# Attention with a linear memory, and a layer of experts: one PSUM bank per head for the joint outputs, two transposes in later slots, and an operand updated in place

## The chip, the core and the metric

The program runs on one core of a Trainium2 chip. The metric is the device time of one execution in microseconds. All matrix products take fp32r operands that are split into a high and a low part, so a product of two fp32 matrices is three matmuls (high·high, high·low, low·high).

## The reference

```python
# q, k, v: [4, 8, 576, 64]; M_prev: [4, 8, 64, 64]; z_prev: [4, 8, 64]
scores = where(causal, -1e9, scale * q @ k.T)
a = softmax(scores)
local = a @ v
q_p = phi(q)                                   # elu(q) + 1
mem_out = (q_p @ M_prev) / (q_p @ z_prev + 1e-6)
g = sigmoid(beta)
x = (g * mem_out + (1 - g) * local)            # -> [2304, 512], heads side by side
p = domain_probs / sum(domain_probs)
out = sum over 4 experts e of p[:, e] * (relu(x @ w1[e]) @ w2[e])   # w1: 512x1024
```

## The kernel before

The attention's rows are cut into chunks of 128 queries (the fifth has 64). A task is one pair of heads of one batch with a run of chunks. Four tasks of batch 0 come first, written out by hand; then come twelve **joint** tasks (batches 1 to 3, four head pairs, chunks 0 and 1), and sixteen tasks of the other chunks (2, 3, 4). A task's steps are called events: `t_trq` and `t_trk` transpose queries and keys on TensorE into a PSUM tile (`tq`, `tk`), `t_trqp` phi of the queries (`tp`), and each is followed by ScalarE and VectorE instructions that write the high and low halves (qa, qb, kha, khb, kl, qpa, qpb); `j_qk` makes the scores (tile `sp`), `j_norm` normalizes, `j_pt` transposes the probabilities (`pt`) and writes their high half with ScalarE (line 604) and low half with VectorE (line 605); `j_o` makes the output (`o`) from phi, the memory `ms`, the probabilities and `v`; `o_out` adds its two halves into the tile `xr`, which holds x.

Meanwhile TensorE works on the experts, with the x that is there: `mm1` (line 968) makes `h`, whose relu is split into `hh` (ScalarE) and `hl` (VectorE, line 978), and `mm2` (line 1000) makes `y`, which VectorE adds into `acc`. The weights of each phase are split by `w_prep`: w2's high half on ScalarE, its low half `w2l` on GpSimd (line 227). These products are cut into parts; a planner puts the events between the parts. Each event has a slot and a priority in a table, and a weight worked out from its cost on TensorE and VectorE; a joint task has four slots, the others five. So the order of a slot's events is by priority, and how many product parts stand between two events goes by the weights.

PSUM tiles come from pools with a few banks per tag, taken in turn: a new tile waits until the instructions that read the tile that had the bank are done. Tag "to" has two banks; `tq`, `tk`, `tp`, the outputs `o`, and at the end two operands of the last pass use them. "qk" has two, "pt" one, "moe" three.

The last pass over the remaining rows computes its products by a scheme with differences of x: `x_steps` makes the operands t1 = x1 − x0, t2 = x3 − t1, t4 = x2 − t2 and t3 = x3 − x1 with `diff`, two halves each, and splits each into high and low (lines 1089 and 1092). They are made while the phase before the pass still runs.

Of the kernel before, what the change touches and what calls it, by code (L numbers as in the profile page):

```python
# [8 lines left out]
F32 = mybir.dt.float32  # L9
# [17 lines left out]
    "trq": [-3, 6.5],  # L27
    "trk": [-4, -0.5],
    "v": -2,
    "trqp": [2, 2.5, -1],  # L30
    "qk": 0,
    "exp": 6.5,
    "norm": 2.3,
# [2 lines left out]
    "jn": [1, -0.5],  # L36
    "jp": [2, 6.4],
    "jo": [3, 11],
    "wpe": 0.5,
    "wvec": 100.0,  # L40
    "frac": 0.97,
# [8 lines left out]
def tile_attention_moe(  # L50
# [13 lines left out]
    nc = tc.nc  # L64
# [542 lines left out]
    def j_o(i):  # L607
        s = slots[i]
        t = s.t
        o = to_tile(f"o{i}").rearrange("p (h q) -> p h q", h=2)  # L610
        for hd in range(2):
            hs = slice(2 * hd, 2 * hd + 2)
            ms = bdat[t.run][2][:, t.a, hs].rearrange("p j d -> p (j d)")
            qp = t.qk["qpa" if hd == 0 else "qpb"]
            nc.tensor.matmul(o[:, hd], lhsT=ms, rhs=qp[:, 0:GW], start=True, stop=False)  # L615
            for x in "hl":
                for j in range(2):
                    vs = t.v[:, j, hs].rearrange("p j d -> p (j d)")
                    nc.tensor.matmul(  # L619
                        o[:, hd, j * P :],  # L620
                        lhsT=vs,
                        rhs=s.p4[x][:, hd, j, j * P :],
                        start=False,
                        stop=j == 1 and x == "l",
                    )
        o_out(t, i, [(0, o[:, 0]), (1, o[:, 1])])

    def o_out(t, i, os_):

        tmp = att.tile([P, NQ], F32, tag="otmp", name=f"otmp{i}", bufs=1)  # L630
        lohi = (slice(0, D), slice(D, P))
        for h, o in os_:
            nc.scalar.activation(tmp[lohi[h], 0 : t.nq], o[lohi[1 - h], 0 : t.nq], AF.Copy)
        if not t.joint:
            a = 3 * P - t.q0
            for h, o in os_:
                x = lohi[h]
                nc.vector.tensor_tensor(
                    tmp[x, a : t.nq], o[x, t.nq : 2 * t.nq - a], tmp[x, a : t.nq], ALU.add
                )  # L640
        runs = []
        for c in t.cs:
            r, a, n = rcol(t.b, c), c * P - t.q0, rows(c)
            if runs and runs[-1][0] + runs[-1][2] == r:
                runs[-1][2] += n
            else:
                runs.append([r, a, n])
        for h, o in os_:
            x = lohi[h]
            for r, a, n in runs:  # L650
                nc.vector.tensor_tensor(
                    xr[x, t.a, r : r + n], o[x, a : a + n], tmp[x, a : a + n], ALU.add
                )

    def s_qk(i):
        s = slots[i]
# [126 lines left out]
    def s_o(i):  # L783
        s = slots[i]
        t = s.t
        pt = PT[s.hd]
        o = to_tile(f"o{i}")
        hs = slice(0, 2) if s.hd == 0 else slice(2, 4)
        ms = bdat[t.run][2][:, t.a, hs].rearrange("p j d -> p (j d)")
        qp = t.qk["qpa" if s.hd == 0 else "qpb"]  # L790
        nc.tensor.matmul(o[:, 0 : t.nq], lhsT=ms, rhs=qp[:, 0 : t.nq], start=True, stop=False, skip_group_check=True)  # L791
        vs = [t.v[:, j, hs].rearrange("p j d -> p (j d)") for j in range(t.nk)]
        a3 = 3 * P - t.q0
        o3 = o[:, a3 : 2 * t.nq - a3].rearrange("p (z q) -> p z q", z=2)
        for x, j in (("h", 0), ("h", 1), ("h", 2), ("h", 4), ("l", 0), ("l", 1), ("hl", 3), ("l", 2)):
            a = max(0, j * P - t.q0)
            nc.tensor.matmul(  # L797
                o3 if j == 3 else o[:, a : t.nq],
                lhsT=vs[j],
                rhs=PTB[s.hd][:, :, 3, a:] if j == 3 else pt[x][:, j, a : t.nq],  # L800
                start=False,
                stop=j == 3 or (x, j) == ("l", 2),
                skip_group_check=True,
            )
        o_out(t, i, [(s.hd, o)])

    def mm(n):
        return max(107.0, n / 2.4 + 2.5)
# [7 lines left out]
    def dv(n):  # L816
        return 150.0 + n / 0.96

    seen = set()
    for t in tasks:  # L820
        s0 = t.s0
        ld = -9 + t.i if t.i < 2 else s0 - 7
        PQ = PR
        n = len(t.cs)
        if t.run not in seen:
            seen.add(t.run)
            ev(s0 - 9, 9 if t.i else 6, lambda r=t.run: batch_load(r))
            ev(s0 - (5 if t.i else 8), 9, lambda r=t.run: batch_load_m(r))
            ev(s0 + (2 if t.joint else 3), 9 if t.joint else 0.1, lambda r=t.run: batch_prep(r))
            if t.cs == CB and t.b == 0:  # L830
                for i in range(2):
                    ev(s0 - 12, 9, lambda i=i: zeros(i))
        if t.joint:
            ev(ld, 6.3, lambda t=t: t_load(t))
        else:
            ev(s0 - 8, 8, lambda t=t: t_load(t, "qk"))
            ev(s0 - 6, 8, lambda t=t: t_load(t, "v"))
        if t.i:
            p1, p2 = (PQ["phi1"], PQ["phi2"]) if t.i > 1 else ((-4, 6.75), (-4, 7))
            ev(s0 + p1[0], p1[1], lambda t=t: t_phi1(t))  # L840
            ev(s0 + p2[0], p2[1], lambda t=t: t_phi2(t), 0.0, dv(n * P))
        ev(
            s0 + (PQ["phi3"][0] if t.i > 1 else (0, -3)[t.i]),
            PQ["phi3"][1] if t.i > 1 else (6.6, 19)[t.i],
            lambda t=t: t_phi3(t),
            0.0,
            600.0 if t.joint else 750.0,
        )
        ev(s0 - 3 if t.i else s0, 20 if t.i else 6.7, lambda t=t: t_phi4(t))
        if t.i == 0:  # L850
            ev(s0 - 1, 5, lambda t=t: t_trq(t), 109.0 * n, 2 * dv(n * P))
        else:
            ev(s0 + PQ["trq"][0], PQ["trq"][1], lambda t=t: t_trq(t), 109.0 * n, 2 * dv(n * P))
            ev(
                s0 + PQ["trk"][0],
                PQ["trk"][1],
                lambda t=t: t_trk(t),
                109.0 * (t.nk - t.k0),
                2 * dv((4 - t.k0) * P),
            )  # L860
        if not t.joint:
            ev(s0 + PQ["trq"][0] + 1, 0.5, lambda t=t: t_cpq(t))
            ev(s0 + PQ["trk"][0], 2.4, lambda t=t: t_cpk(t))
        if t.joint:
            ev(s0 + 1, 9, lambda t=t: t_keep(t))
        elif t.b:
            ev(s0 + PQ["trk"][0], 2.3, lambda t=t: t_take(t))
        ev(s0, PQ["v"], lambda t=t: t_v(t))
        ev(
            s0 + PQ["trqp"][0 if t.joint else 2],  # L870
            PQ["trqp"][1],
            lambda t=t: t_trqp(t),
            109.0 * n,
            2 * dv(t.nq),
        )
    for i, s in slots.items():
        w = wid(s.c)
        t = s.t
        if t.joint:
            ev(i, PQ["qk"], lambda i=i: j_qk(i), 4 * mm(w), 2 * dv(w) + 160)  # L880
            ev(i, PQ["exp"], lambda i=i: j_exp(i))
            ev(i + PQ["jn"][0], PQ["jn"][1], lambda i=i: j_norm(i), 0.0, 2 * dv(w) + 700)
            ev(i + PQ["jp"][0], PQ["jp"][1], lambda i=i: j_pt(i), 218.0 * (s.c + 1), dv(2 * w))
            if i in t.end:
                ev(
                    i + PQ["jo"][0],
                    PQ["jo"][1],
                    lambda i=i: j_o(i),
                    6 * mm(GW) + 4 * mm(P),
                    2 * dv(GW),  # L890
                )
            continue
        ev(i, PQ["qk"], lambda i=i: s_qk(i), 2 * mm(w) if w <= 512 else 6 * mm(w // 2), dv(w))
        ev(i, PQ["exp"], lambda i=i: s_exp(i))
        ev(i + 1, PQ["norm"], lambda i=i: s_norm(i), 0.0, 1000.0 if s.c > 2 else 400.0)
        if s.c == 2:
            ev(i + 1, 6.45, lambda i=i: s_scale(i))
        ev(i + 2, PQ["pt"], lambda i=i: s_pt(i), 109.0 * min(s.c + 1, 4), dv(min(w, 512)))
        if s.c == 4:
            ev(i + 2, PQ["pt"] + 0.1, lambda i=i: s_pt(i, True), 109.0, 400.0)  # L900
        if i in t.end:
            cost = mm(t.nq) + sum(2 * mm(t.nq - max(0, j * P - t.q0)) for j in range(t.nk))
            ev(i + 3, PQ["o"], lambda i=i: s_o(i), cost, 600.0)
# [177 lines left out]
    def x_steps():  # L1081
# [10 lines left out]
            eng.tensor_tensor(x[n][1][:, c], src(), f(x[n][0][:, c]), ALU.subtract)  # L1092

        def diff(n, c, tag, a, b_):
            t_[n, c] = ps.tile([P, 512], F32, tag=tag, name=f"{n}_{c}", bufs=2)
            nc.vector.tensor_tensor(t_[n, c], a(), b_(), ALU.subtract)

        V, G = nc.vector, nc.gpsimd
# [24 lines left out]
        both(D_, "t4", "qk", 2, "t2")  # L1123
        both(L_, "t2", "t2", V)
        both(H_, "t4", "t4")
        both(D_, "t3", "to", 3, 1)
        both(L_, "t4", "t4", V)
        both(H_, "t3", "t3")
        both(L_, "t3", "t3", V)
# [660 lines left out]
```

## Time and profile before

| what | value |
| --- | --- |
| time, median of 3 runs | 975.38 us (975.23 to 976.3) |
| the profiled execution: its time | 975.54 us |
| its span in the trace | 973.8 us |
| TensorE busy | 967.5 us (99%) |
| VectorE busy | 663.0 us (68%) |
| ScalarE busy | 569.6 us (58%) |
| GpSimd busy | 591.1 us (61%) |

The profile comes from one execution; its span in the trace is a little shorter than its time. Shares are of the span. Matmuls are pipelined, so their durations overlap: what one costs is read from the distance between the starts of neighbours.

### The profile page before, as it was taken

What the parts mean: (1) busy time and instruction counts of PE and PEld (TensorE: products, weight loads), DVE (VectorE), ACT (ScalarE), POOL (GpSimd) and SP (SyncE); (2) the same over time, 40 slices, a digit from 0 to 9 for tenths busy, and PEclk for the clock granted to TensorE, in tenths of its full rate; (3) what the DMA queues carried; (4) which work ended last, traced back from release to release, by engine and by line L of the source; (5) the groups of instructions that cost most, each with busy time, mean ns of one, the idle gap of its engine ahead of it and who ended that gap; (6) DMA issues with size and microseconds to landing.
All of it is one profiled execution on the core that took longest, in us unless ns stands there. A gap on an engine that the chain in (4) does not pass through costs nothing.

```text
span 973.8 us, 16241 instructions
## 1 busy us (share of the span) xinstructions
PE 967.5 (99%) x5018; PEld 815.2 (84%) x5018; DVE 663.0 (68%) x1791; ACT 569.6 (58%) x1393; POOL 591.1 (61%) x621
## 2 busy tenths in 40 slices
PE   9999999999999999999999999999999999999998
PEld 6889888888888899888888888888888888888887
DVE  7888888889888788888888877834324243342533
ACT  7888776776766779766666675643424334242430
POOL 7999856765674668865557455676255372554720
PEclk9999999999999999999999999999999999999999
DMA  8679655654444267644535332242111111111102
GB/s 193 187 186 225 163 160 142 175 146 110 116 126 126 65 185 201 178 124 115 131 106 134 94 95 64 64 130 60 50 44 55 54 55 55 44 55 47 51 1 87
DMA packets 187815, 107.04 MB, mean 110 GB/s; under 512 B 90704, under 2 KB 167632, under 8 KB 187728
## 3 DMA queue, kind: packets, MB, share of 16 engines
q1 hardware_dynamic: 186608, 105.73, 40.1%
q8 instruction: 40, 0.66, 0.3%
q14 instruction: 47, 0.39, 0.1%
q10 hardware_dynamic: 1088, 0.26, 0.1%
q0 software_dynamic: 32, 0.00, 0.0%
HBM read 93.23 MB, written 8.13 MB: 104 GB/s over the span
## 4 chain that ended last, share of the span: by engine, by line
PE 97%; DVE 1%; POOL 1%; DMA 1%; issue 0%; ACT 0%; SPq 0%; POOLq 0%
PE y L1000 23%; PE h L968 22%; PE y L1277 18%; PE x L1199 9%; PE z L1199 5%; PE pt L364 4%; PE sp L678 4%; PE o L797 4%; PE y L1199 2%; PE o L619 1%; PE tp L364 1%; PE tq L364 1%; PE tk L364 1%; PE sp L533 1%; PE o L791 0%; PE o L615 0%
## 5 line engine op out<-in xcount | busy, mean ns | idle before, releaser
L227 POOL TENSOR_TENSOR w2l<-stg,w2h 128x512 fp32r<-128x512 f32 x128 | 167.5, 1316 | 149.1 <-ACT w2h L224 144.7
L968 PE MATMUL h<-xh,w 128*128 128x512 f32 (+1 forms) x768 | 243.9, 368 | 0.0
L227 POOL TENSOR_TENSOR w<-stg,w 128x512 fp32r<-128x512 f32 x96 | 124.9, 1308 | 141.8 <-ACT w L224 132.3
L968 PEld LDWEIGHTS h<-xh,w 128*128 128x128 f32 x768 | 138.7, 189 | 17.8 <-issue 0.2
L968 PE MATMUL h<-xl,w 128*128 128x512 f32 (+1 forms) x384 | 136.3, 355 | 0.0
L1000 PE MATMUL y<-w2h,hh 128*128 128x512 f32 x320 | 134.4, 420 | 0.0
L1000 PE MATMUL y<-w2h,hl 128*128 128x512 f32 x320 | 126.1, 394 | 0.2 <-DVE hl L978 0.2
L1000 PE MATMUL y<-w2l,hh 128*128 128x512 f32 x320 | 125.7, 393 | 0.3 <-POOL w2l L227 0.3
L1294 DVE SCALAR_TENSOR_TENSOR acc<-y,pn,acc 128x512 f32<-128x512 f32 (+1 forms) x57 | 41.6, 740 | 82.2 <-PE y L1277 82.2
L735 ACT ACTIVATE pt<-pt 128x384 fp32r<-128x384 f32 (+3 forms) x128 | 50.2, 420 | 62.8 <-PE pt L364 61.2
L968 PEld LDWEIGHTS h<-xl,w 128*128 128x128 f32 x384 | 72.8, 190 | 5.8
L1000 PEld LDWEIGHTS y<-w2h,hl 128*128 128x128 f32 x320 | 60.0, 188 | 14.0 <-DVE hl L978 0.6
L977 ACT ACTIVATE hh<-h 128x512 fp32r<-128x512 f32 (+1 forms) x96 | 50.3, 524 | 29.2 <-PE h L968 27.7
L1000 PEld LDWEIGHTS y<-w2l,hh 128*128 128x128 f32 x320 | 60.5, 189 | 8.1 <-POOL w2l L227 1.1
L1000 PEld LDWEIGHTS y<-w2h,hh 128*128 128x128 f32 x320 | 60.3, 188 | 7.8
L737 DVE TENSOR_TENSOR pt<-pt,pt 128x384 fp32r<-128x384 f32 (+3 forms) x128 | 57.3, 468 | 11.0 <-ACT pt L735 9.7
L978 DVE SCALAR_TENSOR_TENSOR hl<-h,hh 128x512 fp32r<-128x512 f32 (+1 forms) x96 | 57.5, 599 | 10.3 <-ACT hh L977 9.1
L364 PE MATMUL pt<-ident,s 128*128 128x128 f32 (+1 forms) x376 | 60.8, 272 | 0.2
L1223 DVE TENSOR_TENSOR cp_a<-y,cp_a 128x512 f32<-128x512 f32 x16 | 11.1, 692 | 71.4 <-PE y L1199 71.4
L364 PEld LDWEIGHTS pt<-ident,s 128*128 128x128 f32 (+1 forms) x376 | 46.9, 139 | 14.2 <-issue 0.5
L224 ACT ACTIVATE w<-stg 128x512 fp32r<-128x512 f32 x92 | 57.0, 625 | 0.8
L1016 DVE SCALAR_TENSOR_TENSOR acc<-y,pn,acc 128x512 f32<-128x512 f32 x70 | 52.3, 747 | 5.9 <-PE y L1000 5.0
(291 smaller groups left out, 2503.7 us busy)
## 6 DMA issues: line engine op xcount, KB each, us to landing
stg<-in_moe_w_dram SPq DMA_DIRECT2D x256, 256.0 KB, 3.0
natall<-in_v_dram SPq DMA_DIRECT2D x32, 128.0 KB, 3.4
natall<-in_q_dram SPq DMA_DIRECT2D x60, 64.0 KB, 3.0
out_dram<-acc SPq DMA_DIRECT2D x15, 256.0 KB, 2.1
natall<-in_k_dram SPq DMA_DIRECT2D x52, 64.0 KB, 2.4
zb<-in_z_prev_dram SPq DMA_DIRECT2D x7, 256.0 KB, 4.2
mr<-in_M_prev_dram SPq DMA_DIRECT2D x14, 128.0 KB, 3.2
natall<-in_v_dram SPq DMA_DIRECT2D x24, 64.0 KB, 2.4
```

The lines of the kernel that those rows point to most:

```text
L224: nc.scalar.activation(hi, t, AF.Copy)
L227: nc.gpsimd.tensor_tensor(lo, t, f(hi), ALU.subtract)
L364: nc.tensor.transpose(dst, src, ident[0:n, 0:n])
L735: nc.scalar.activation(dh, src, AF.Copy)
L737: nc.vector.tensor_tensor(dl, src, f(dh), ALU.subtract)
L968: nc.tensor.matmul(pt[0][:, cols], lhsT=w_[:, c], rhs=x_[:, c, cols], start=(c == 0 and z == 0), stop=(c == NKD - 1 and z == 2),)
L977: nc.scalar.activation(h_, pt[0][:, cols], AF.Relu)
L978: nc.vector.scalar_tensor_tensor(l_, pt[0][:, cols], 0.0, f(h_), ALU.max, ALU.subtract)
L1000: nc.tensor.matmul(pt[0], lhsT=h_[fc][:, tk], rhs=w_, start=(fc == 0 and z == 0), stop=(fc == HF - 1 and z == 2),)
L1016: nc.vector.scalar_tensor_tensor(acc[g, tt], pt[0], pe, acc[g, tt], ALU.mult, ALU.add)
L1199: nc.tensor.matmul(k_, lhsT=w_[:, c], rhs=x_[:, c], start=new and n == 0, stop=n == 5, skip_group_check=True,)
L1277: nc.tensor.matmul(y0, lhsT=a[:, tk], rhs=w_[:, x0:x1], start=(fc == 0 and z == 0), stop=(fc == HF - 1 and z == 2),)
```

## The change

It has three parts. `j_o` takes a "to" bank for each head (o{i}_0, o{i}_1) where both heads had one bank. In a head's bank, columns 0 to 255 hold the memory product and chunk 0's values times the high, then the low half of the probabilities; for chunk 1 the high and the low half stand side by side in one operand of 256 columns, whose product goes to columns 128 to 383. So there are four matmuls of 256 columns for each head instead of three of 256 and two of 128, and an add on VectorE joins the last 128 columns to the rest. `o_out` is called for each head. `t_trq` of the joint tasks goes from slot −3, priority 6.5, to slot −2, priority 1, counted from the task's first slot, and their `t_trqp` from slot +2 to slot +3. In `x_steps`, t3 is made as t2 − x0 in t2's own PSUM bank, instead of x3 − x1 in a bank of its own.

```diff
-    "trqp": [2, 2.5, -1],
+    "trqp": [-1, 2.5],
+    "jtrq": [-2, 1],
+    "jtrqp": [3, 2.5],
...
     def j_o(i):
...
-        o = to_tile(f"o{i}").rearrange("p (h q) -> p h q", h=2)
+        both = PTB[t.i % 2].rearrange("p z j q -> p z (j q)")
+        tmp = o_tmp(i)
         for hd in range(2):
+            o = to_tile(f"o{i}_{hd}")
...
-            nc.tensor.matmul(o[:, hd], lhsT=ms, rhs=qp[:, 0:GW], start=True, stop=False)
-            for x in "hl":
-                for j in range(2):
-                    vs = t.v[:, j, hs].rearrange("p j d -> p (j d)")
-                    nc.tensor.matmul(
-                        o[:, hd, j * P :],
-                        lhsT=vs,
-                        rhs=s.p4[x][:, hd, j, j * P :],
-                        start=False,
-                        stop=j == 1 and x == "l",
-                    )
-        o_out(t, i, [(0, o[:, 0]), (1, o[:, 1])])
+            v0, v1 = (t.v[:, j, hs].rearrange("p j d -> p (j d)") for j in range(2))
+            c1 = (2 * hd + 1) * GW + P
+            o1 = o[:, P : P + GW].rearrange("p (z q) -> p z q", z=2)
+            for n, (dst, w_, x_) in enumerate(
+                (
+                    (o[:, 0:GW], ms, qp[:, 0:GW]),
+                    (o[:, 0:GW], v0, s.p4["h"][:, hd, 0]),
+                    (o1, v1, both[:, :, c1 : c1 + P]),
+                    (o[:, 0:GW], v0, s.p4["l"][:, hd, 0]),
+                )
+            ):
+                nc.tensor.matmul(
+                    dst, lhsT=w_, rhs=x_, start=n == 0, stop=n > 1, skip_group_check=True
+                )
+            o_out(t, hd, o, tmp)
...
-        if not t.joint:
-            a = 3 * P - t.q0
...
+        a = P if t.joint else 3 * P - t.q0
+        nc.vector.tensor_tensor(
+            tmp[x, a : t.nq], o[x, t.nq : 2 * t.nq - a], tmp[x, a : t.nq], ALU.add
+        )
...
-                    6 * mm(GW) + 4 * mm(P),
-                    2 * dv(GW),
+                    8 * mm(GW),
+                    2 * dv(GW) + 2 * dv(P),
...
         def diff(n, c, tag, a, b_):
-            t_[n, c] = ps.tile([P, 512], F32, tag=tag, name=f"{n}_{c}", bufs=2)
+            if tag:
+                t_[n, c] = ps.tile([P, 512], F32, tag=tag, name=f"{n}_{c}", bufs=2)
+            else:
+                t_[n, c] = a()
             nc.vector.tensor_tensor(t_[n, c], a(), b_(), ALU.subtract)
...
-        both(D_, "t3", "to", 3, 1)
+        both(D_, "t3", None, "t2", 0)
```

How the order moves is seen best in three places. The first is TensorE's order where the joint tasks end: the tile tq is that of the first task with three chunks (its three transposes), o the output of the eleventh joint task, h the experts' first product. Before:

```order
L364 MATMUL tq_2920<-ident,natall 128x128 x3
L968 MATMUL h_0_2901<-xh,w_111 128x512
L968 MATMUL h_0_2901<-xl,w_111 128x512
L968 MATMUL h_0_2901<-xh,w_111 128x512
L615 MATMUL o_2957<-qpa_84,ms_0_2440 128x256
L619 MATMUL o_2957<-pt_98,v_2652 128x256
L619 MATMUL o_2957<-pt_98,v_2652 128x128
L619 MATMUL o_2957<-pt_98,v_2652 128x256
L619 MATMUL o_2957<-pt_98,v_2652 128x128
L615 MATMUL o_2957<-qpb_85,ms_0_2440 128x256
L619 MATMUL o_2957<-pt_98,v_2652 128x256
```

And of the change:

```order
L366 MATMUL tq_2946<-ident,natall 128x128 x3
L972 MATMUL h_1_2935<-xh,w_111 128x512
L972 MATMUL h_1_2935<-xl,w_111 128x512
L972 MATMUL h_1_2935<-xh,w_111 128x512 x2
L972 MATMUL h_1_2935<-xl,w_111 128x512
L972 MATMUL h_1_2935<-xh,w_111 128x512
L630 MATMUL o_0_2987<-qpa_84,ms_0_2444 128x256
L630 MATMUL o_0_2987<-pt_98,v_2675 128x256 x3
L630 MATMUL o_1_2995<-qpb_85,ms_0_2444 128x256
L630 MATMUL o_1_2995<-pt_98,v_2675 128x256 x3
```

The output now stands six products behind tq instead of three, has eight matmuls, and takes two tiles, o_0 and o_1, right behind tq in the tag's turn.

The second place is TensorE's order at the output of the second joint task; tq is that of a later joint task. Before:

```order
L968 MATMUL h_3_1121<-xh,w_111 128x256
L968 MATMUL h_3_1121<-xl,w_111 128x256
L968 MATMUL h_3_1121<-xh,w_111 128x256
L364 MATMUL tq_1131<-ident,natall 128x128 x2
L968 MATMUL h_3_1121<-xh,w_111 128x256
L968 MATMUL h_3_1121<-xl,w_111 128x256
L968 MATMUL h_3_1121<-xh,w_111 128x256 x2
L968 MATMUL h_3_1121<-xl,w_111 128x256
L968 MATMUL h_3_1121<-xh,w_111 128x256 x2
L968 MATMUL h_3_1121<-xl,w_111 128x256
L968 MATMUL h_3_1121<-xh,w_111 128x256
L615 MATMUL o_1156<-qpa_93,ms_0_763 128x256
```

And of the change:

```order
L972 MATMUL h_3_1122<-xh,w_111 128x256
L972 MATMUL h_3_1122<-xl,w_111 128x256
L972 MATMUL h_3_1122<-xh,w_111 128x256
L630 MATMUL o_0_1139<-qpa_93,ms_0_753 128x256
L630 MATMUL o_0_1139<-pt_99,v_795 128x256 x3
L630 MATMUL o_1_1147<-qpb_94,ms_0_753 128x256
L630 MATMUL o_1_1147<-pt_99,v_795 128x256 x3
L972 MATMUL h_3_1122<-xh,w_111 128x256
L972 MATMUL h_3_1122<-xl,w_111 128x256
L972 MATMUL h_3_1122<-xh,w_111 128x256 x2
```

The transposes of tq are no longer ahead of the output (they stand among later products), and the output comes eight rows earlier in the expert products of h_3.

The third is VectorE's order where the operands of the last pass are made; t2, t3 and t4 are PSUM tiles, each with its half's number, and t2l and t4l the low halves. Before:

```order
L1092 TENSOR_TENSOR t2l_8274<-t2_0_8339,t2h_8273 128x512
L1092 TENSOR_TENSOR t2l_8274<-t2_1_8344,t2h_8273 128x512
L978 SCALAR_TENSOR_TENSOR hl2_109<-h23_2_8381,hh2_105 128x512
L1096 TENSOR_TENSOR t3_0_8412<-xr_100 128x512
L1096 TENSOR_TENSOR t3_1_8417<-xr_100 128x512
L1092 TENSOR_TENSOR t4l_8280<-t4_0_8372,t4h_8279 128x512
```

And of the change:

```order
L1096 TENSOR_TENSOR t2l_8286<-t2_0_8351,t2h_8285 128x512
L1096 TENSOR_TENSOR t2l_8286<-t2_1_8356,t2h_8285 128x512
L982 SCALAR_TENSOR_TENSOR hl2_109<-h23_2_8393,hh2_105 128x512
L1103 TENSOR_TENSOR t2_0_8351<-t2_0_8351,xr_100 128x512
L1103 TENSOR_TENSOR t2_1_8356<-t2_1_8356,xr_100 128x512
L1096 TENSOR_TENSOR t4l_8292<-t4_0_8384,t4h_8291 128x512
```

The two subtractions stand at the same place; they now read and write t2's tile where they read two pieces of xr.

## Rows read from the trace of the kernel before

**Rows 1.** The head of the page: the span, busy time by engine, granted TensorE clock
```profile
span 973.8 us, 16241 instructions
...
PE 967.5 (99%) x5018; PEld 815.2 (84%) x5018; DVE 663.0 (68%) x1791; ACT 569.6 (58%) x1393; POOL 591.1 (61%) x621
...
PEclk9999999999999999999999999999999999999999
```

**Rows 2.** TensorE's waits: us in total, times, longest
```profile
PE ids L1610 <- DVE hh L1656: 1.5, 1, 1.5
PE y L1000 <- POOL w2l L227: 0.3, 1, 0.3
```

**Rows 3.** Timeline of TensorE, 63.3 to 66.5: start, duration, line, tiles
```profile
63.50 0.28 PE L615 MATMUL o<-qpa,ms 128*128 128x256 f32 x1
...
64.62 0.45 PE L1000 MATMUL y<-w2h,hh 128*128 128x512 f32 x1
64.91 0.40 PE L1000 MATMUL y<-w2l,hh 128*128 128x512 f32 x1
65.14 0.40 PE L1000 MATMUL y<-w2h,hl 128*128 128x512 f32 x1
...
66.07 0.28 PE L533 MATMUL sp<-kha,qa 128*128 128x256 f32 x1
66.19 0.28 PE L533 MATMUL sp<-qz,qa 128*128 128x256 f32 x1
```

**Rows 4.** Line 615: ns min/median/max, first and last start
```profile
L615 PE MATMUL o<-qpa,ms x12: 277/282/283, 49.6 to 207.2; 128*128 128x256 f32 x12
```

**Rows 5.** Timelines of GpSimd and TensorE, 47 to 62
```profile
47.64 5.08 POOL L227 TENSOR_TENSOR w2l<-stg,w2h 128x512 fp32r<-128x512 f32 x4
...
49.00 0.50 PE L1000 MATMUL y<-w2l,hh 128*128 128x512 f32 x1 [0.27 <-POOL w2l L227]
...
52.82 0.45 PE L1000 MATMUL y<-w2l,hh 128*128 128x512 f32 x1
...
61.41 1.30 POOL L227 TENSOR_TENSOR w2l<-stg,w2h 128x512 fp32r<-128x512 f32 x1
```

**Rows 6.** Timelines of TensorE, ScalarE and VectorE, 189.5 to 194.2
```profile
189.94 0.49 PE L364 MATMUL tq<-ident,natall 128*128 128x128 f32 x3
...
190.96 0.28 PE L615 MATMUL o<-qpa,ms 128*128 128x256 f32 x1
...
190.47 0.38 ACT L376 ACTIVATE qa<-tq 64x256 fp32r<-64x256 f32 x1 [1.73 <-PE tq L364]
...
192.24 0.42 DVE L380 SCALAR_TENSOR_TENSOR qa<-tq,qa 64x256 fp32r<-64x256 f32 x1 [1.00 <-ACT khb L390]
...
193.81 0.23 DVE L396 TENSOR_TENSOR kl<-tq,khb 64x64 fp32r<-64x64 f32 x1
```

**Rows 7.** The tile otmp, instructions by line
```profile
L638 DVE TENSOR_TENSOR otmp<-o,otmp x32: 340/355/361, 227.5 to 616.1; 64x192 f32<-64x192 f32 x32
```

**Rows 8.** Timelines of TensorE and VectorE behind the first two chunk-1 transposes
```profile
43.92 0.87 PE L364 MATMUL pt<-ident,s 128*128 128x128 f32 x4
...
46.87 0.69 DVE L605 TENSOR_TENSOR pt<-pt,pt 128x512 fp32r<-128x512 f32 x1
...
59.26 0.60 PE L364 MATMUL pt<-ident,s 128*128 128x128 f32 x4
...
61.77 0.69 DVE L605 TENSOR_TENSOR pt<-pt,pt 128x512 fp32r<-128x512 f32 x1 [1.05 <-ACT pt L604]
```

**Rows 9.** Timelines of VectorE and TensorE, 622 to 635
```profile
622.65 1.28 DVE L1096 TENSOR_TENSOR t<-xr,t 128x512 f32<-128x512 f32 x2
...
629.81 2.85 DVE L1096 TENSOR_TENSOR t<-xr 128x512 f32<-128x512 f32 x2
...
633.36 0.39 PE L1000 MATMUL y<-w2l,hh 128*128 128x512 f32 x1
633.90 0.50 PE L1000 MATMUL y<-w2h,hl 128*128 128x512 f32 x1 [0.15 <-DVE hl L978]
634.24 0.39 PE L1000 MATMUL y<-w2h,hh 128*128 128x512 f32 x1
```

More of the change, by code (lines that the diff above doesn't have):

```diff
@@ L614, in j_o, with o_tmp, o_out @@
             qp = t.qk["qpa" if hd == 0 else "qpb"]
-            nc.tensor.matmul(o[:, hd], lhsT=ms, rhs=qp[:, 0:GW], start=True, stop=False)
-            for x in "hl":
-                for j in range(2):
-                    vs = t.v[:, j, hs].rearrange("p j d -> p (j d)")
-                    nc.tensor.matmul(
-                        o[:, hd, j * P :],
-                        lhsT=vs,
-                        rhs=s.p4[x][:, hd, j, j * P :],
-                        start=False,
-                        stop=j == 1 and x == "l",
-                    )
-        o_out(t, i, [(0, o[:, 0]), (1, o[:, 1])])
[L628 to L633, printed above, removed]
-        if not t.joint:
-            a = 3 * P - t.q0
[L636 to L639, printed above, removed]
-                )
+            v0, v1 = (t.v[:, j, hs].rearrange("p j d -> p (j d)") for j in range(2))
[7 more added lines that the diff above has]
+                    (o[:, 0:GW], v0, s.p4["l"][:, hd, 0]),
+                )
+            ):
[3 more added lines that the diff above has]
+            o_out(t, hd, o, tmp)
+    def o_tmp(i):
+        return att.tile([P, NQ], F32, tag="otmp", name=f"otmp{i}", bufs=1)
+    def o_out(t, h, o, tmp):
+        x, y = (slice(0, D), slice(D, P))[:: 1 - 2 * h]
+        nc.scalar.activation(tmp[x, 0 : t.nq], o[y, 0 : t.nq], AF.Copy)
+        a = P if t.joint else 3 * P - t.q0
+        nc.vector.tensor_tensor(
+            tmp[x, a : t.nq], o[x, t.nq : 2 * t.nq - a], tmp[x, a : t.nq], ALU.add
+        )
         runs = []
@@ L647, in o_out @@
                 runs.append([r, a, n])
[L648 to L653, printed above, removed]
+        for r, a, n in runs:
+            nc.vector.tensor_tensor(
+                xr[x, t.a, r : r + n], o[x, a : a + n], tmp[x, a : a + n], ALU.add
+            )
     def s_qk(i):
@@ L804, in s_o @@
             )
-        o_out(t, i, [(s.hd, o)])
+        o_out(t, s.hd, o, o_tmp(i))
     def mm(n):
@@ L852, in tile_attention_moe @@
         else:
-            ev(s0 + PQ["trq"][0], PQ["trq"][1], lambda t=t: t_trq(t), 109.0 * n, 2 * dv(n * P))
+            x = PQ["jtrq" if t.joint else "trq"]
+            ev(s0 + x[0], x[1], lambda t=t: t_trq(t), 109.0 * n, 2 * dv(n * P))
             ev(
@@ L868, in tile_attention_moe @@
         ev(s0, PQ["v"], lambda t=t: t_v(t))
+        x = PQ["jtrqp" if t.joint else "trqp"]
         ev(
-            s0 + PQ["trqp"][0 if t.joint else 2],
-            PQ["trqp"][1],
+            s0 + x[0],
+            x[1],
             lambda t=t: t_trqp(t),
```

## The prediction

> **What bounds the kernel now.** I read the head of the page first. TensorE is busy for 967.5 of the 973.8 us of the span, and its granted clock stands at the upper level, 2.4 GHz, in every slice [rows 1]. So what the change is worth is read in TensorE's own stream: time that a shorter set of matmuls takes out of it, and time that a wait puts in. The view of TensorE's waits shows how little is left to remove: only two of its five entries are above 0.25 us, and the 1.5 us one is in the first microseconds, which the change doesn't touch [rows 2]. A shorter set of matmuls is worth its full length where TensorE is the bound, and nothing where TensorE stands at another engine's heel. I then went to the four places that the change touches, each in the timeline of its engines.
>
> **Joint outputs: ten matmuls become eight.** A block of ten is followed best from its first start to the second product behind it, since the product behind the block is slow too: block from 63.50, y from 64.62, next y from 64.91 and one more from 65.14 [rows 3]. An ordinary 512-column product takes 65.14 − 64.91 = 0.23, the one behind the block 64.91 − 64.62 = 0.29, so the block costs 64.62 − 63.50 + (0.29 − 0.23) = 1.18 us. The new block is eight matmuls of 256 columns with the same 2048 columns in all. Two 256-column matmuls in a row start 66.19 − 66.07 = 0.12 apart [rows 3], so eight cost 0.96. That gives 0.22 us a task; what makes a 128-column matmul dear is that it isn't half as long as one of 256. The bounds are 0 (128 columns at half of 0.12: 6 × 0.12 + 4 × 0.06 = 0.96) and 0.22; the rows show the ten at 1.18, so I take 0.22.
> The Trainium skill, "TensorE: Matmul & The Clock Gate", section "Back-to-back issue gap", gives 134 cycles for a single 128-column matmul and 262 for 256, and 81 ns as a sustained figure at 128 that includes weight loads. By its isolated figures the block would go from 0.88 to 0.87, by the sustained one from 0.98 to 0.87, so that the twelve would save 0.1 to 1.3 us. The 1.18 of this trace is above both, so the trace decides.
>
> There are twelve joint tasks, whose output blocks start from 49.6 to 207.2 [rows 4]. **The first saves nothing.** There GpSimd's low half of w2 is the bound: four pieces run without a gap from 47.64 for 5.08 us, to 52.72. TensorE waits for the first at 49.00 and uses the fourth at 52.82, 0.10 us after it is made [rows 5]. The saving of the block between them turns into a longer wait for GpSimd. In the next phase the first piece is ready at 61.41 + 1.30 = 62.71 and used at 64.91, so 2.2 us of slack [rows 3, 5]. So 11 × 0.22 = **−2.4**.
>
> **Own banks: a new wait where the joint tasks end.** The two banks of tag "to" go round. Before, a joint output took one; now it takes two in a row, and the second needs the bank of whatever stood in the ring two allocations earlier. In the joint run that is, as a rule, a tile long read. At the switch to the runs of three chunks it isn't: the tq of the thirteenth task (three transposes) stands right ahead of the eleventh joint output, so the output's first head takes tk's bank and its second head takes tq's, whose readers have just begun. In before the same tq starts at 189.94, ScalarE starts to read it at 190.47, VectorE only at 192.24, behind ScalarE's last eviction (khb), and the last reader is kl at 193.81 + 0.23 = 194.04: 4.10 us after tq [rows 6]. In the new order three more 512-column products stand between tq and the block: the first head is due 190.96 − 189.94 = 1.02 plus 3 × 0.23 = 1.71 after tq, the second 4 × 0.12 later at 2.19. Wait: 4.10 − 2.19 = 1.9 us. Bounds: 0.7, if VectorE orders kl ahead of the other readers and has no other work (it can't start before 192.24 and needs 0.42 and 0.23 [rows 6], so 2.9 after tq), and 2.6, if the first head's three new VectorE and ScalarE instructions come between. I take **+1.9**. Elsewhere in the joint run some ten 512-column products or their like, 2.4 us at 0.23, lie between a second head and the tile that takes its bank; the copy and the two adds that free it fit there.
>
> **VectorE's extra work.** Each head gets one more add (128 columns on 64 partitions); the nearest rows are those of the three-chunk outputs, 0.355 for 192 columns [rows 7], so about 0.3, 24 times: 7 us spread over some 165, on an engine that is busy for 663.0 of 973.8 [rows 1]. It costs nothing by itself, but see the second rival. If VectorE had no room it would cost at most 7 us.
>
> **Transposes a slot later.** Twelve blocks in 157.6 us [rows 4] make a task 14.3 us and a slot 3.6. The queries' transposes now stand two slots less a little ahead of their first use, about 7 us, against 4.1 that their readers take [rows 6]; phi's stand over two slots ahead of the output, about 8. MoE products hide both. Nothing is taken for them. A slip would show in the score products' start, by the amount over 7. The changed cost weights move all of this by up to a few MoE products, the same in number.
> They do one more thing: the queries' transposes no longer stand between the second chunk's pt and the output (second fence of the order), and the block comes nearer. Before, the pt at 59.26 has 4.2 us to the block at 63.50, and its low half is made at 61.77 + 0.69 = 62.46, 3.2 after pt, of which 1.05 was a wait for ScalarE [rows 3, 8]. In the new order 21 products of 256 columns at 0.12 and the four transposes (some 0.4) stand between the second task's pt and its output, 2.9 us, and by the same count the others have 2.5 to 3.2; the low half is read 0.24 later, by the third matmul. For the first task the low half comes 46.87 + 0.69 − 43.92 = 3.64 after pt [rows 8]; its wait of some 0.6 vanishes in the GpSimd bound. For the second I take 0.2, for the rest together 0.1: **+0.3**, bounds 0 and 2.8 (0.25 in each of eleven).
>
> **The operand updated in PSUM.** t3 = x3 − x1 with two SBUF operands takes 2.85 us for its two halves while GpSimd works; t2 just before, with one operand in PSUM, takes 1.28 [rows 9]. The hl behind it is late, and TensorE's product, due at 633.36 + 0.23 = 633.59, starts at 633.90, the next at 634.24 instead of 633.82 [rows 9]: 0.42 lost. t3 = t2 − x0 has one operand in PSUM: 1.57 us earlier, and the wait goes. **−0.4**, bounds −0.4 and 0 (if something else is late in its place).
>
> **Sum.** −2.4 + 1.9 + 0.3 − 0.4 = −0.6 against the profiled execution of 975.54, which is 0.16 above the median of 975.38: 975.38 − 0.6 = **974.8**.
>
> **Rivals.** 1. *The wait at the switch is not there, or short* (kl read early, or the tiles fall otherwise): −2.4 − 0.4 + 0.3 = −2.5, 972.9. Against it: the order of banks follows from the order of allocations, and VectorE starts on tq 2.3 us after tq for a reason that stays (ScalarE's evictions) [rows 6]. For it: the time of VectorE's queue there is of the old order. 0.20.
> 2. *VectorE falls behind between pt and the output*, in each joint task: it has the two new adds, norm, phi's low halves, which now come a slot later, and the low half of pt in one stretch, and the block needs that last. Then the low half ends over 3 us after pt again, and TensorE stands at it eleven times. At 0.25 us a task (2.8 in all) the saving is gone and the time is 977.3; at 0.4 a task it is 975.38 − 2.4 + 1.9 − 0.4 + 4.4 = 978.9. For it: the 3.2 at 59.26 [rows 8]. Against: a third of that was ScalarE's lateness, in a phase with weights to prepare. 0.12, slower.
> 3. *The block saves nothing*, by the sum with 128 columns at half the time of 256, as the page above has it: −0.4 + 1.9 + 0.3 = +1.8, 977.2. The 1.18 speaks against it. 0.03.
>
> **How the numbers follow.** The forecast has 0.65. About 0.2% (some 2 us: 973.4 to 977.3) is what a measurement of this kernel tells from no change; the forecast lies inside it with most of its range, 973.4 to 976.3. The first rival is faster, 0.20, and a little of the forecast's edge; the second is slower, and a part of the third: 0.14 with the mishaps that I don't see. So faster 0.20, same 0.66, slower 0.14. The range reaches from the first rival's 972.9, less 0.1, to the forecast with its wait at 2.6 and more behind pt, 977.0; what lies outside is mostly the second rival.
>
> **What would show each step.** The joint block takes 0.96 from its start to the matmul behind it, and 128-column rows of o are gone. The new profile's waits of TensorE have an entry "o <- DVE kl" of about 1.9 us near 190 us, once. If it is absent, rival 1. Waits of o on pt's low half (DVE) in each joint task: rival 2. At the transition t3 takes about 1.3 for both halves and no y waits for hl. TensorE uses the fourth piece of w2's low half at about 52.8, as before. The forecast is wrong if the wait at the switch is under 0.5 or over 3, or if pt's low half comes later than 3.2 us after pt in most tasks.

## The result and the profile after

The changed kernel takes 981.12 us (median of 6 runs, 980.18 to 983.56), against 975.83 for the kernel before (6 runs, 975.23 to 976.54). The ratio is 1.0055, 95% interval 1.0045 to 1.0066: 5.3 us slower, where 974.8 and a range to 977.0 were forecast. The profiled executions' spans differ by 979.6 − 973.8 = 5.8.

The head of the page after, which answers to [rows 1]:

```profile
span 979.6 us, 16216 instructions
...
PE 967.3 (99%) x4994; PEld 813.4 (83%) x4994; DVE 669.4 (68%) x1815; ACT 570.3 (58%) x1393; POOL 589.1 (60%) x621
```

There are 24 matmuls less, 24 VectorE instructions more. TensorE's busy time is the same within 0.2, so it doesn't show the saving (in run 9, where no output waits, it is 965.9); the span is longer, so TensorE waits more. TensorE's waits after (us in total, times, longest), beside [rows 2]:

```profile
PE o L630 <- DVE kl L398: 2.2, 1, 2.2
PE y L1004 <- POOL w2l L229: 1.5, 1, 1.5
PE ids L1617 <- DVE hh L1663: 1.5, 1, 1.5
PE o L630 <- DVE pt L607: 1.1, 3, 0.6
PE tq L366 <- ACT hh L981: 0.9, 1, 0.9
```

Only the third of these stands in [rows 2] at its size. The forecast has the first; the second has no place in it, the fourth is there with a fraction of its size, the fifth was excluded. Matmuls overlap, so the view's idle time is less than what a wait costs; I size each below by starts: the distance between two neighbours less their usual 0.23 (512 columns) or 0.12 (256).

**The block.** Timeline of TensorE, second head of an output, beside [rows 3]:

```profile
92.44 0.28 PE L630 MATMUL o<-qpb,ms 128*128 128x256 f32 x1
92.56 0.52 PE L630 MATMUL o<-pt,v 128*128 128x256 f32 x3
92.92 0.28 PE L972 MATMUL h<-xh,w 128*128 128x256 f32 x1
93.04 0.27 PE L972 MATMUL h<-xl,w 128*128 128x256 f32 x1
```

Four matmuls take 92.92 − 92.44 = 0.48, and the one behind them 0.12 as usual. The eight cost 0.96, as forecast.

**The switch.** Timelines of TensorE and VectorE where the joint tasks end, beside [rows 6]:

```profile
194.39 0.49 PE L366 MATMUL tq<-ident,natall 128*128 128x128 f32 x3
...
196.23 0.52 PE L630 MATMUL o<-pt,v 128*128 128x256 f32 x3
198.97 0.36 PE L630 MATMUL o<-qpb,ms 128*128 128x256 f32 x1 [2.21 <-DVE kl L398]
...
197.02 0.42 DVE L382 SCALAR_TENSOR_TENSOR qa<-tq,qa 64x256 fp32r<-64x256 f32 x1
...
198.59 0.23 DVE L398 TENSOR_TENSOR kl<-tq,khb 64x64 fp32r<-64x64 f32 x1
```

The second head, due at 196.23 + 3 × 0.12 = 196.59, starts at 198.97: 2.4 us, behind the last reader of tq (kl, to 198.82).

**pt's low half.** Timelines of TensorE, ScalarE and VectorE at the third output, beside [rows 8]:

```profile
74.14 0.60 PE L366 MATMUL pt<-ident,s 128*128 128x128 f32 x4
...
77.21 0.28 PE L630 MATMUL o<-pt,v 128*128 128x256 f32 x1
77.72 0.51 PE L630 MATMUL o<-pt,v 128*128 128x256 f32 x2 [0.23 <-DVE pt L607]
...
75.83 0.63 ACT L226 ACTIVATE w2h<-stg 128x512 fp32r<-128x512 f32 x1 [0.44 <-DMA stg<-in_moe_w_dram]
76.36 0.58 ACT L606 ACTIVATE pt<-pt 128x512 fp32r<-128x512 f32 x1
...
76.98 0.69 DVE L607 TENSOR_TENSOR pt<-pt,pt 128x512 fp32r<-128x512 f32 x1 [1.03 <-ACT pt L606]
```

The third matmul, the first that reads the low half, is 77.72 − 77.21 − 0.12 = 0.39 late. ScalarE stood behind a piece of w2 that had not landed, so it copied the high half only 2.2 us after pt, and VectorE waited for that. By the same difference of starts, four outputs (the third, fourth, fifth and seventh) lose 0.39, 0.26, 0.42 and 0.78: 1.85 us.

A late piece of w2 stands ahead of the first two only. At the fifth and the seventh, which lose 1.20 of the 1.85, ScalarE is done early and VectorE is late by its own queue. At the seventh:

```profile
132.90 0.87 PE L366 MATMUL pt<-ident,s 128*128 128x128 f32 x4
...
137.38 0.51 PE L630 MATMUL o<-pt,v 128*128 128x256 f32 x2 [0.62 <-DVE pt L607]
...
133.81 0.60 ACT L606 ACTIVATE pt<-pt 128x512 fp32r<-128x512 f32 x1 [1.04 <-PE pt L366]
...
133.31 0.42 DVE L382 SCALAR_TENSOR_TENSOR qpa<-tp,qpa 64x256 fp32r<-64x256 f32 x1
...
136.64 0.69 DVE L607 TENSOR_TENSOR pt<-pt,pt 128x512 fp32r<-128x512 f32 x1
```

The high half is ready at 133.81 + 0.60 = 134.41. From phi's low half (qpa) at 133.31 to pt's low half at 136.64 VectorE works without a break, and pt's low half ends 4.4 us after pt, where in the trace of before it ends 2.0 after. Phi's low halves, which the change moved a slot later, take 0.9 us of that stretch; how much of the delay is theirs alone no run tests.

**tq at the output's bank.** Timelines of ScalarE, VectorE and TensorE behind the fourth output:

```profile
94.66 0.78 ACT L640 ACTIVATE otmp<-o 64x256 f32<-64x256 f32 x2
...
95.39 0.42 DVE L653 TENSOR_TENSOR xr<-o,otmp 64x256 f32<-64x256 f32 x1
...
95.91 0.41 PE L366 MATMUL tq<-ident,natall 128*128 128x128 f32 x2 [0.94 <-ACT hh L981]
```

The tq comes 1.9 us behind the output's end and takes its first head's bank, whose last reader (xr) ends at 95.81. Due 0.12 behind the matmul at 94.69, it loses 95.91 − 94.81 = 1.1. I take xr for its releaser and not hh, which the row names: hh writes no bank of tag "to". Run 7's trace agrees: three times there a tq starts 0.1 behind the end of such an xr (80.98, 109.64 and 137.81).

**w2's low half.** Timelines of TensorE and GpSimd:

```profile
394.20 0.47 PE L1004 MATMUL y<-w2h,hh 128*128 128x512 f32 x1
396.20 0.50 PE L1004 MATMUL y<-w2l,hh 128*128 128x512 f32 x1 [1.52 <-POOL w2l L229]
...
394.87 1.28 POOL L229 TENSOR_TENSOR w2l<-stg,w2h 128x512 fp32r<-128x512 f32 x1
```

This one, 396.20 − 394.20 − 0.23 = 1.8 us, lies among the tasks of three chunks, none of whose steps the change edits.

**The transition.** t3's two halves take 1.29 us, and TensorE's products go on at 0.23, beside [rows 9]:

```profile
636.07 1.29 DVE L1103 TENSOR_TENSOR t<-t,xr 128x512 f32<-128x512 f32 x2
...
638.26 0.39 PE L1004 MATMUL y<-w2l,hh 128*128 128x512 f32 x1
638.49 0.39 PE L1004 MATMUL y<-w2h,hl 128*128 128x512 f32 x1
```

### The profile page after: what moved, and what is told of

The parts are those of the page before. It is cut to its first block, busy times and chain, and to the rows that moved or that the text cites. A ratio compares the mean times of both kernels' runs of the same rounds, so it can differ in the third digit from the quotient of the medians.

```text
span 979.6 us, 16216 instructions
## 1 busy us (share of the span) xinstructions
PE 967.3 (99%) x4994; PEld 813.4 (83%) x4994; DVE 669.4 (68%) x1815; ACT 570.3 (58%) x1393; POOL 589.1 (60%) x621
## 4 chain that ended last, share of the span: by engine, by line
PE 85%; DVE 4%; POOL 4%; issue 2%; DMA 2%; ACT 2%; SPq 1%; POOLq 0%; DVEq 0%; ACTq 0%
PE h L972 18%; PE y L1004 18%; PE y L1284 18%; PE x L1206 9%; PE z L1206 4%; PE sp L680 4%; PE o L799 3%; PE pt L366 3%; PE y L1206 2%; DMA stg<-in_moe_w_dram 2%; POOL w2l L229 2%; POOL w L229 1%; PE o L630 1%; PE tq L366 1%; PE tp L366 1%
```

## The experiments

Theory A: the eight matmuls and t3 save what was forecast, and the loss lies in the ring of two banks, in the slots, and in the order that the planner's new weights make. Rival B: the new form of the output itself (its adds, the banks) puts VectorE behind, or the waits come by chance of one execution.

**1. slots_only: the new slots alone**

```diff
-            ev(s0 + PQ["trq"][0], PQ["trq"][1], lambda t=t: t_trq(t), 109.0 * n, 2 * dv(n * P))
+            x = (-2, 1) if t.joint else PQ["trq"]
+            ev(s0 + x[0], x[1], lambda t=t: t_trq(t), 109.0 * n, 2 * dv(n * P))
...
-            s0 + PQ["trqp"][0 if t.joint else 2],
+            s0 + (3 if t.joint else -1),
```

> The kernel before with one part of the change: the joint tasks' tq in slot -2 and tp in slot +3; outputs, weights of the planner and t3 as before. Theory A (the new slots bring the output so near behind pt that TensorE waits for pt's low half): waits of o on VectorE's pt, 1 to 2 us in all, no wait of 2 us near 190 us, time about 977.3. Rival B (the slots are harmless, the two new adds on VectorE make the low half late): no such waits, 975.8 as before.

978.27 us against 975.84, ratio 1.0024 (1.0015 to 1.0033). Its waits have no kl and no w2l, but:

```profile
PE o L619 <- DVE pt L605: 0.9, 3, 0.3
```

The slots alone bring the waits for pt's low half, without an add on VectorE. That part of rival B falls; what is left of it is VectorE's queue with phi's low halves, which move with the slots. They cost 2.4 us, more than the 1.5 expected.

**2. old_weights: the changed kernel with the planner's old weights**

```diff
-                    8 * mm(GW),
-                    2 * dv(GW) + 2 * dv(P),
+                    6 * mm(GW) + 4 * mm(P),
+                    2 * dv(GW),
```

> The changed kernel with the planner's old weights for the joint outputs, so that every step of the three-chunk tasks stands among the expert products exactly where it stood before. Theory A (the wait of 1.8 us for w2's low half near 394 us comes from the order that the new weights make): that wait is gone, the others stay, about 979.4. Rival B (it comes from the later joint part or from the transfers of one execution): it stays, 981.1.

979.05 us, ratio 1.0035 (1.0023 to 1.0047). That is 2.1 less than the changed kernel. The wait for w2l near 394 us is gone, that for pt stays (0.9 in three places), and so does that for kl (2.6, once).

**3. tq_behind_output: the three-chunk run's first tq behind the output**

```diff
-            x = PQ["jtrq" if t.joint else "trq"]
+            x = PQ["jtrq" if t.joint or t.i == 12 else "trq"]
...
-            ev(s0 + PQ["trq"][0] + 1, 0.5, lambda t=t: t_cpq(t))
+            ev(s0 - 2, 1.5 if t.i == 12 else 0.5, lambda t=t: t_cpq(t))
```

> The changed kernel with one move: tq of the first three-chunk task stands behind the eleventh joint output (slot -2, as the joint ones) and the copy that needs it half a priority later. Theory A (the output's second head waits for the bank of that tq): the wait of 2.2 us near 196 us is gone, 978.9, up to 0.9 more if tq then waits for the output's own readers. Rival B (VectorE is simply behind there, whatever the bank): a wait of about 2 us stays with another name, 981.1.

978.76 us, ratio 1.0029 (1.0018 to 1.0041): 2.4 less than the changed kernel, and no wait for kl. That for w2l (1.5, once) is there unchanged, and those for pt's low half add up to the same (1.1 in three places, not all at the same outputs). The tq behind the fourth output loses only 0.4 here, where it lost 1.1: that size is of one execution.

**4. banks_old_slots: the changed kernel with the joint tasks' old slots** (`"jtrq": [-3, 6.5]`, `"jtrqp": [2, 2.5]`)

> The changed kernel with tq and tp of the joint tasks in their old slots. Theory A (the ring of two banks: an output's second head takes the bank of whatever stood just ahead of it, here tq in nearly every joint task, 1.4 us ahead where its readers take 4): a wait of 2 to 3 us in each of some eleven tasks, about 1003 in all. Rival B (the wait near 196 us is peculiar to the switch to three chunks): 981 or below, since pt's low half has more time again.

995.72 us (one run), less than the 1003 expected. Waits for tq's readers at eleven of the twelve outputs, ten for qb and one of 1.9 for kl:

```profile
PE o L630 <- DVE qb L385: 13.6, 10, 2.0
```

So the ring is the rule, not the switch: with a bank per head from this ring the old slots can't be kept, and the move of the slots is what the banks make necessary. There is no wait for pt's low half here, which with run 1 leaves that wait to the slots.

**5. weights_only: the kernel before with the new weights** (the lines of run 2, the other way round)

> The kernel before with the planner's new weights for the joint outputs and nothing else. Theory A (the order that these weights make in the three-chunk tasks makes w2's low half late): one wait of y for w2l of 1.5 to 1.8 us near 390 us that the kernel before doesn't have, time about 977.6. Rival B (it comes from what else the change does to the joint part): no such wait, 975.8.

980.22 us against 975.88, ratio 1.0045 (1.0032 to 1.0057). New weights in the planner, and not an instruction more or less in the tasks, cost 4.3 us where 1.8 was expected:

```profile
PE y L1000 <- DVE hl L978: 1.9, 2, 1.6
PE y L1000 <- POOL w2l L227: 1.7, 2, 1.5
```

The wait for w2l is there, at 392 us. So is one for hl of 1.7 at 638, where t3 still reads two SBUF operands; that I had not expected. The changed kernel has the same weights and not this wait: its t3 is made in PSUM. Across all the programs, the wait for w2l of 1.5 near this place is in the four with the new weights (after, runs 3, 4 and 5) and in none of the others.

How the order does it shows in GpSimd's queue ahead of that place. Before (w is w1's low half, v the split of a later task's values):

```profile
374.83 5.08 POOL L227 TENSOR_TENSOR w<-stg,w 128x512 fp32r<-128x512 f32 x4
379.87 0.73 POOL L481 TENSOR_SCALAR v<-natall 128x640 fp32r<-128x640 f32 x1
...
382.22 2.88 POOL L227 TENSOR_TENSOR w2l<-stg,w2h 128x512 fp32r<-128x512 f32 x2
```

And of the change, at the same products some 3.9 us later:

```profile
380.83 3.82 POOL L229 TENSOR_TENSOR w<-stg,w 128x512 fp32r<-128x512 f32 x3
...
385.55 2.58 POOL L229 TENSOR_TENSOR w2l<-stg,w2h 128x512 fp32r<-128x512 f32 x2 [0.91 <-ACT w2h L226]
388.09 0.73 POOL L483 TENSOR_SCALAR v<-natall 128x640 fp32r<-128x640 f32 x1
```

Before, v fills the time in which ScalarE makes w2's high halves. Now GpSimd idles for 0.91 there, and v stands between the second and the third low half. The last split of w1 ends at 384.65 instead of 379.91 + 3.9 = 383.8, since two short steps of a task (rn and qp, from 379.86) stand between the first and the second split of w1, where they stood ahead of all four. These 0.8 and 0.9 are about the 1.8 that TensorE waits. SyncE's loads move too, but neither ScalarE nor GpSimd waits for a transfer between 366 and 397 us in this trace. That the weights cause the wait is shown; that it goes by this queue is read from the rows and wasn't tried by itself.

**6. old_weights_tq_behind: the cures of runs 2 and 3 together**

> The changed kernel with both cures that were tried apart: the planner's old weights (−2.1) and the first three-chunk tq behind the eleventh joint output (−2.4). Theory A (the two waits are independent): 981.1 − 2.1 − 2.4 = 976.6, neither wait there; the waits for pt's low half stay, some 1.7 us. Rival B (they feed each other, or a wait moves to the next place): 978 or more.

976.68 us, ratio 1.0009 (1.0000 to 1.0018). The effects add up, and 4.4 of the 5.3 us are gone. The waits for pt's low half stay (1.3 in four places by the view of the waits).

**7. pt_earlier: and chunk 1's transposes ahead of the slot's score products**

```diff
-            ev(i + PQ["jp"][0], PQ["jp"][1], lambda i=i: j_pt(i), 218.0 * (s.c + 1), dv(2 * w))
+            x = (2, -0.2) if s.c else PQ["jp"]
+            ev(i + x[0], x[1], lambda i=i: j_pt(i), 218.0 * (s.c + 1), dv(2 * w))
```

> As old_weights_tq_behind, and the transposes of chunk 1's probabilities stand ahead of the slot's score products, so that TensorE has 4.0 to 4.4 us of work between pt and the output, as before the change (2.5 to 3.3 with it). Theory A (the distance alone makes the waits for the low half): they go, 1.7 us less, 974.9, faster than the kernel before. Rival B (VectorE's new adds push its queue back by as much): waits of 0.3 to 0.8 stay in four tasks, 976.6.

977.33 us, ratio 1.0013 (1.0005 to 1.0022): no gain. The entry for the low half is gone, but others stand in its place:

```profile
PE pt L366 <- DVE s L578: 0.8, 2, 0.4
...
PE tq L366 <- ACT hh L982: 0.4, 1, 0.4
```

The earlier pt now waits for the normalized probabilities, and tq at the output's bank. Theory A has the waits for the low half right, and its time wrong. My reading, which no run tests by itself, is that the chain from scores to output is as long as its slots, so that what one step gains the next gives back.

**8. pt_earlier_ten_matmuls: run 7 with the output of the kernel before**

> As pt_earlier, but with the joint output of the kernel before: one bank for both heads, ten matmuls, no adds. Theory A (the eight matmuls save 0.22 us a task): 2.4 us slower than pt_earlier, about 977.3 if that has 974.9. Rival B (a 128-column matmul is worth half of one of 256): as fast as pt_earlier or faster, since the adds are gone.

977.32 us, ratio 1.0015 (1.0006 to 1.0024): the same as run 7, where 2.4 more was expected. By medians, the own banks bring nothing in this arrangement (the two profiled executions are 1.2 us apart in span, 975.1 and 976.3). In run 7's trace their tq waits, which this kernel's doesn't; an output of this kernel waits for pt instead (0.4 and 0.3). So I looked for an arrangement in which they bring no such wait.

**9. second_head_in_qk: old slots, old weights, and the second head in a bank of another tag**

```diff
-            o = to_tile(f"o{i}_{hd}")
+            o = ps.tile([P, 512], F32, tag=("to", "qk")[hd], name=f"o{i}_{hd}", bufs=2)
```

> The changed kernel with the second head's output in a bank of the scores' tag qk, the first head's in tag to, and with that the old slots of tq and tp and the planner's old weights: the eight matmuls and the adds stay, and t3 in PSUM. Theory A (the loss is all in the ring of banks and in what was moved because of it; the eight matmuls save 0.22 us a task, t3 0.4): no new wait, 975.9 − 2.4 − 0.4 = 973.1, faster than the kernel before. Rival B (the adds and the later release of otmp cost VectorE's chain what TensorE saves): 975.5 to 976.5, with waits on VectorE in the joint tasks.

974.85 us against 977.13 on that chip, ratio 0.9973 (0.9963 to 0.9984): faster than the kernel before beside it, and 1.8 above the 973.1 expected. Of its waits one is longer than in the kernel before:

```profile
PE y L1004 <- DVE hl L982: 0.4, 1, 0.4
```

It costs 0.6 by starts, at 83.0 us. The adds are all in it, and no output waits. Since its order is that of the kernel before, the same transposes can be compared. Before:

```profile
101.50 0.60 PE L364 MATMUL pt<-ident,s 128*128 128x128 f32 x4
...
202.52 0.60 PE L364 MATMUL tk<-ident,natall 128*128 128x128 f32 x4
```

And in this run:

```profile
102.07 0.60 PE L366 MATMUL pt<-ident,s 128*128 128x128 f32 x4
...
201.59 0.60 PE L366 MATMUL tk<-ident,natall 128*128 128x128 f32 x4
```

From 0.57 behind to 0.93 ahead: 1.50 us in seven tasks, 0.21 each (the wait for hl lies ahead of them).

**10. t3_only: the kernel before with t3 in t2's bank**

> The kernel before with t3 made in t2's bank and nothing else. Theory A: the wait of y for hl near 633.6 us goes, 0.4 us less, 975.4; the subtraction's two halves take 1.3 us instead of 2.85. Rival B (something else is late in its place): 975.9.

975.54 us, ratio 0.9983 (0.9974 to 0.9992). VectorE's two instructions take 0.69 each and y's wait for hl is gone:

```profile
L1099 DVE TENSOR_TENSOR t<-t,xr x2: 690/690/690, 631.8 to 632.4; 128x512 f32<-128x512 f32 x2
```

The ratio is a gain of 0.8 to 2.5 us, more than the 0.4 that the trace gives; the runs of the kernel before spread from 975.67 to 979.28 on that chip, and what else is in it stays open. The profiled execution of this run, its slowest (977.10), shows one thing that such a spread can hold, with the steps in the order of before. Timeline of ScalarE ahead of the third output:

```profile
77.64 0.63 ACT L224 ACTIVATE w2h<-stg 128x512 fp32r<-128x512 f32 x1 [3.42 <-DMA stg<-in_moe_w_dram]
```

A piece of w2 landed late, pt's high half stood behind it, and the output lost 1.3 us at the high half and 0.4 at the low. So a wait for pt can come by the chance of one execution in the old order too; what run 1's median of eleven executions shows is that the new slots cost 2.4.

Because of the spread I read runs 9 and 10 beside each other: 0.7 us between their medians is what the eight matmuls are seen to bring there, not 2.4.

## Why the prediction was wrong

| term | forecast | measured in the profile after |
| --- | --- | --- |
| eight matmuls, eleven tasks | −2.4 | −2.4 by the block's 0.96; 0.21 a task in run 9 |
| second head at tq's bank | +1.9 | +2.4 |
| outputs at pt's low half | +0.3 | +1.85 |
| later tiles at the output's banks | 0 | +1.1 |
| planner's weights | 0 | +1.8 |
| first phase, to the fourth w2l | 0 | +0.4 (53.26, where [rows 5] have 52.82); 0.3 of it not by the change |
| t3 in PSUM | −0.4 | −0.4 |

That makes +4.75 of the 5.8 between the spans; the other 1.1 lies in gaps of under 0.3 that I have not assigned. The experts' first product starts at 26.96 after and 26.65 before, ahead of any step that the change moves, so 0.3 of the 5.8 is of these two executions.

- **The step that failed outright** is "the changed cost weights move all of this by up to a few MoE products, the same in number", taken at nothing. The number is the same, but the other engines' steps have their places among those products, GpSimd's splits among them. Runs 2 and 5 show it: 2.1 us in the changed kernel by the medians (1.8 at w2l in its trace), 4.3 alone. The move reached tasks that the diff doesn't name.
- **The output near pt** was sized at +0.3 because the low half of the second task, at 3.2 us, was taken as the worst. Run 1 shows the mechanism without the rest. The distances came out (2.96 where 2.9 was forecast for the second task, 2.5 to 3.5 for those up to the tenth); the low half's time did not. ScalarE's wait for a piece of w2, which I put down to one phase and held against the second rival, comes back at two more outputs. The other two, 1.20 of the 1.85, are VectorE's queue with phi's low halves in it, at 4.4 us after pt in the worst.
- **"the copy and the two adds that free it fit there"** fails once: the ScalarE copy stood behind such a piece too, and tq came 1.9 us behind the output, for its first head's bank, where I had counted 2.4 between.
- **The wait at the switch** was right in place, cause and name, and 0.5 short: the tq readers stood behind the normalization on VectorE (197.02, though ScalarE was done with tq at 196.69 by its rows). Run 3 shows the cause. The rest of the 0.5 lies between kl's end at 198.82 and TensorE's start at 198.97.
- **The block, the first task at GpSimd's heel and t3** were right. The Trainium skill, "TensorE: Matmul & The Clock Gate", section "Back-to-back issue gap", was not the better guide: by an estimate from its single-matmul gaps ten and eight would cost the same (0.88 and 0.87). Run 9 shows 0.21 a task.
- Of the rivals, the second was the nearest: its waits are there, in four tasks of eleven, and with 1.85 us below the 2.8 that it asked for. Two of the four are its mechanism, VectorE with phi's low halves a slot later; the adds that it also named aren't needed (run 1). The wait of tq and the weights' order were in no rival, so that 0.14 for slower was too low. None of the signs that the prediction set for being wrong came true: the wait at the switch was 2.4, and the low half came later than 3.2 us in five tasks of twelve, not in most.

## What to carry to other kernels

A number that a planner weighs is an edit of every later instruction: look at what each engine's queue holds ahead of the next step that TensorE needs, in the new order, before pricing it at nothing. Two tiles from a ring of two banks mean that the second stands behind whatever was allocated last, so count who reads that tile still, or take the second from a ring with slack. When a move shortens one distance in a chain of engines, price the chain at its worst task, with all that its engines have queued ahead of it and with transfers that land late, not at one task's rows.

## What the runs showed of the hardware

A wait of TensorE can cost more than its length. In run 2's trace the output's second head waits until 195.16. The windows around it (us, busy of each engine, granted clock, DMA share, GB/s):

```profile
192.00:195.10 3.10, 0.60 (x5) 0.39 (x3) 2.17 (x11) 2.92 (x11) 2.94 (x5) 0.95 0.80 198
195.10:198.20 3.10, 3.04 (x9) 2.67 (x10) 1.97 (x5) 0.66 (x2) 2.93 (x5) 0.50 0.49 115
198.20:204.00 5.80, 5.80 (x32) 4.76 (x31) 3.24 (x13) 3.19 (x10) 3.53 (x3) 1.00 0.83 202
```

Behind the wait the granted clock stands at 0.50, 1.2 GHz, for 3.1 us, and 512-column products start 0.43 apart; then it is back at 2.4 GHz. Four 256-column and five 512-column matmuls take 3.1 us there where 4 × 0.12 + 5 × 0.23 = 1.6 is usual: 1.5 us on top of the wait of 2.7. The profile after, with a wait of 2.4 in the same place, kept 1.00. In run 4's trace the clock falls behind two of the eleven waits, 2.0 and 1.9 long by the view of the waits, where that of the profile after is 2.2. So what a wait of about 2 us costs can't be told from its length. Of the changed kernel's six executions, the two with a mean granted clock of 0.998 are the slowest (982.16 and 983.56); the four at 1.000 lie between 980.18 and 981.33. The Trainium skill, "TensorE: Matmul & The Clock Gate", section "What's actually happening", says that the clock is at the lower level after idleness. That the waits at three places brought it there, and the one of the profile after did not, is what these traces show.

VectorE's subtraction with two SBUF operands took 2.85 for two halves [rows 9], from 629.81 on, and 2 × 0.69 with one operand in PSUM (run 10, from 631.8 on). GpSimd's splits of w2 run beside both. Timelines of GpSimd, before and in run 10:

```profile
627.82 4.28 POOL L227 TENSOR_TENSOR w2l<-stg,w2h 128x512 fp32r<-128x512 f32 x3
...
628.54 5.12 POOL L227 TENSOR_TENSOR w2l<-stg,w2h 128x512 fp32r<-128x512 f32 x4
```

The Trainium skill, "SBUF — State Buffer", section "Who interferes with whom", has the rule for it: two SBUF inputs contend with a GpSimd instruction that reads SBUF, one doesn't. The traces agree.
